# Block-sparse attention with a Fourier mixer: whitened tiles fetched tile by tile, and mask factors kept in memory for TensorE

## The chip, the core and the metric

The kernel runs on one core of one Trainium2 chip. The metric is the time of one execution in device microseconds; three timed runs of the kernel before gave 1060.93, 1061.15 and 1061.73 us, so a median of 1061.15 us. The profile is of one further execution. PE is TensorE's matmul path and PEld its weight loads, DVE is VectorE, ACT is ScalarE, POOL is GpSimd and SP the engine whose queue issues nearly all of the DMAs.

## What is computed

Attention with a block mask over 4 batches, 8 heads, 768 positions and 64 features, and then a mixer over 4 x 768 x 512: a two-dimensional Fourier transform whose real part is added, a normalisation of each row ("whitening"), and two matrix products with a ReLU between them ("channel work").

```python
scores = scale * np.matmul(q, k.transpose(0, 1, 3, 2))
scores = np.where(mask, scores, -1000000000.0)      # blocks of 32: window, edges, 3 sampled
attn = softmax(scores)
x = np.matmul(attn, v) -> (4, 768, 512)
...
X = np.fft.fft(np.fft.fft(x, axis=1), axis=2)
u = x + np.real(X)
un = (u - mean(u)) / np.sqrt(var(u) + 1e-06)
ch = np.maximum(un @ w_ch1, 0.0) @ w_ch2            # 512 -> 2048 -> 512
return u + ch
```

## The kernel before

Attention goes over 16 pairs of heads (4 for each batch); a pair is 6 slots of two units, and a batch is 24 slots, a "phase". A unit is 128 keys against 384 queries for the two heads: 2 score matmuls (L579), a mask, the exponential on ACT (L599, L607) and 2 value matmuls (L653). The profile records each float32 matmul twice, so a slot has 8 records of each line. For the first units, 106 of 192, PE makes the mask itself: 2 more matmuls (L589, one record each) of two bf16 tables of factors, `of_k` and `off_q`, add it to the scores in PSUM. Once `channel_step` has run for the first time `masks["by_pe"]` is false for good; from then on ACT scales and copies the scores (L607) and DVE multiplies the exponentials by a stored mask (L609). The tables' place in the on-chip memory (`factors`) is then used for other things. DVE or POOL also adds up the exponentials for the softmax's denominator (L634, L639), and a group of small steps turns the sums into scaling factors: PE moves them (L738, L751, "N3"), DVE takes the reciprocal (L754) and multiplies the rows of `x` (L766).

The mixer of batch b runs during phase b+1. Its Fourier steps, normalisation and whitening (L956) are small steps in a queue named `apart`, which fill gaps. Whitening gives 6 tiles `un` (2 halves of the 768 positions times 3) of 128 x 512. Each is transposed in 32 x 32 blocks by DVE (L1015) and written to memory (`far`, L1016); after all 6, `un_back` brings them back with 8 DMAs of 192 KB (L1025) into `unT`, so that they stand turned round as a whole. `right` (L1057) then makes four combinations of 128 x 768 on DVE for the channel work, which are held until the planner's time `state["back"]` has passed (a constant `BACK[b]` after the fetch).

Channel work of a batch is a queue `late`: 8 `quad`s, each 7 products of two matmuls (L1103, four records) by the Strassen-Winograd scheme, with sums on DVE (L1108) and ReLUs on ACT (L1112), and four rounds r of outputs, two quads and 6 `channels` to a round. An output round is either 24 matmuls (6 `channels` of 4, 48 records of L1268, with one DVE addition each, L1271) or 21 products of `round_of` (L1211), again Strassen-Winograd; `seven[r]` picks the second where `state["alone"]` was true at the round's first quad, which means that attention stood still (`until`) for the channel work to end. The last round always takes the first form. It is followed by `store` (L1279), 3 or 4 DMAs for each of the 6 tiles of `x`.

Attention of batch b needs the `x` buffers of batch b-2: `place` (L676 on PE, L677 on ACT) writes the first pair of batch b into them, so `until(finished)` runs the whole remaining channel work of b-2 ahead of it. After that there is a stretch of attention without channel work, before the quads of batch b-1 can start (the "dry stretch"). In later pairs `x` is filled by way of memory (`row`, L692, L696).

The instructions of each engine stand in one order, which this program writes as it is built: `when` holds a planned time for each engine, `busy` books work, `gap` fills PE's waits with the first step of `apart` that is due, `do_apart` issues one. SP's DMAs are issued in program order too, and each waits until the one eight before it on SP has landed. Queries and keys (`load_q`, `load_k`, L231) and the turned outputs (L692, L696) go through the same queue.

The lines that the change touches: the tables at L369 to L380, `scores` (L579 to L589), `un_flip` (L998, the last batch alone, which turns its tiles on PE), `un_blocks`, `un_back`, `right`, `quad`'s operands (L1099, L1103), the list `after` of steps of `apart`, `BACK`, `channel_step` and `slot`.

Of the kernel before, what the change touches and what calls it, by code (L numbers as in the profile page):

```python
# [11 lines left out]
FP32 = mybir.dt.float32  # L12
BF16 = mybir.dt.bfloat16
# [86 lines left out]
def kernel(  # L100
# [14 lines left out]
    nc = tc.nc  # L115

    B, H, S, D = q.shape
    DM = H * D
    FF = w_ch1.shape[1]
    P = 128  # L120
    C = S // P
    BLK = 32
    NB = S // BLK
    NR = sampled_blocks.shape[1]
    HS = S // 2
    KS = cos_s.shape[1]
    KD = cos_d.shape[1]
    ND = DM // P
    NF = FF // P
    T = C // 2  # L130
# [51 lines left out]
    tr_p = ctx.enter_context(tc.tile_pool(name="tr_p", bufs=2))  # L182
# [3 lines left out]
    far_p = ctx.enter_context(tc.tile_pool(name="far_p", bufs=1, space=bass.MemoryType.DRAM))  # L186
# [7 lines left out]
    when = {"PE": 0.0, "ACT": 0.0, "DVE": 0.0, "POOL": 0.0}  # L194
# [18 lines left out]
    def room(i, shape, name, dtype=FP32):  # L213
        return big.tile(shape, dtype, tag=f"big{i}", name=name)
# [86 lines left out]
    def bit(n):  # L301
# [5 lines left out]
                      in_=bass.AP(tensor=_words(sampled_blocks, NB * NR), offset=0,  # L307
                                  ap=[[0, NB], [1, 2 * NB * NR]]))
# [30 lines left out]
    factors = room(2, [P, 3, S], "factors", BF16)  # L339
    of_k, off_q, keep_q = (factors[:, i, :] for i in range(3))  # L340
# [5 lines left out]
    def twice(t):  # L346
        nc.vector.tensor_copy(out=t[D:D + NB, :], in_=t[0:NB, :])
# [18 lines left out]
                            op0=ALU.is_equal)  # L366
    spread_q(off_q[0:NB, :], maskT)
    twice(off_q)
    def mask_step(i):  # L369


        half, c = divmod(i, C)
        m, at = ps_m.tile([P, 512], FP32, tag="m", name="m"), bank("m")
        nc.tensor.matmul(m[:, 0:HS], of_k[0:D, c * P:(c + 1) * P],
                         keep_q[0:D, half * HS:(half + 1) * HS], start=True, stop=True)
        done = busy("PE", 0.17) + HOP

        def keep_it():
            nc.scalar.copy(out=mask[:, c, half * HS:(half + 1) * HS], in_=m[:, 0:HS])
            give(at, busy("ACT", 0.5, done))  # L380
        return keep_it
# [62 lines left out]
    for w, w_sb in ((w_ch1, w1_sb), (w_ch2, w2_sb)):  # L444
        rows, cols = w.shape
        words = _words(w, rows * cols)
        for row in range(rows // P):
            for col in range(0, cols, WN):
                src = bass.AP(tensor=words, offset=2 * (row * P * cols + col),
                              ap=[[2 * cols, P], [1, 2 * WN]])  # L450
# [35 lines left out]


    by_pe, to_gather = set(), deque()
    masks = {"by_pe": True}

    turned, e_of, acc_of, o_of, sums_of, x_of, sp_of = {}, {}, {}, {}, {}, {}, {}
    s_at, e_at, e_free, oT_at, acc_at = {}, {}, {}, {}, {}
# [69 lines left out]
    def scores(us):  # L562

        n, w = divmod(us[0], UP)
        half = w // C
        qT, kT = turned[n, 0], turned[n, 1]
        queries = slice(half * HS, (half + 1) * HS)
        got = []
        for u in us:
            c = u % C  # L570
            s = ps_s.tile([P, 2, 512], FP32, tag="s", name="s")
            got.append((u, s))
            if n < NP or masks["by_pe"]:
                by_pe.add(u)
            busy("PE", 0.72, max(e_at.get(u - SLOT, 0.0), z_at[u % 2]))
            s_at[u] = when["PE"] + HOP
            for i in range(2):
                rows = slice(D * i, D * i + D)
                nc.tensor.matmul(s[:, i, 0:HS], kT[rows, c * P:(c + 1) * P], qT[rows, queries],  # L579
                                 start=True, stop=u not in by_pe)  # L580
        for u, s in got:
            if u not in by_pe:
                continue
            c = u % C
            busy("PE", 0.25)
            s_at[u] = when["PE"] + HOP
            for i in range(2):
                rows = slice(D * i, D * i + D)
                nc.tensor.matmul(s[:, i, 0:HS], of_k[rows, c * P:(c + 1) * P], off_q[rows, queries],  # L589
                                 start=False, stop=True)  # L590
        return got

# [390 lines left out]
    def mixer(b, xA, xB):  # L983


        uns, unT = {}, {}
# [2 lines left out]

        def un_flip(half, m):  # L990
            if half not in unT:
                unT[half] = tr_p.tile([P, ND, T * P], FP32, tag="tr", name="unT")
            un = uns.pop((half, m))
            tag, pool = (("t", ps_t), ("m", ps_m))[half == 1 and m != 0]
            tp = pool.tile([P, ND, P], FP32, tag=tag, name="utp")
            for d in range(ND):
                nc.tensor.transpose(tp[:, d, :], un[:, d * P:(d + 1) * P], ident)
            nc.scalar.copy(out=unT[half][:, :, m * P:(m + 1) * P], in_=tp)  # L998

# [3 lines left out]

        lines = {}

        def un_blocks(half, m):  # L1010

            un = uns.pop((half, m))
            if half not in lines:
                lines[half] = far_p.tile([T, P, DM], FP32, tag=f"un{half}", name="far")
            nc.vector.transpose(out=un, in_=un)  # L1015
            nc.sync.dma_start(out=lines[half][m], in_=un)  # L1016

        def un_back():

            for half in range(2):  # L1020
                unT[half] = tr_p.tile([P, ND, T * P], FP32, tag="tr", name="unT")
                of = lines[half].rearrange("m (g j) (k a i) -> a j k (m g) i",
                                           j=BLK, a=P // BLK, i=BLK)
                for a in range(P // BLK):
                    nc.sync.dma_start(  # L1025
                        out=unT[half][BLK * a:BLK * a + BLK].rearrange(
                            "j k (g i) -> j k g i", i=BLK),
                        in_=of[a])
            state["back"] = max(when["PE"], state["ready"]) + BACK[b]

        t, s = {}, {}
        K1, K2 = slice(0, ND // 2), slice(ND // 2, ND)

        def spare_room():
            if s:
                return
            rest, n, w = room(5, [P, ND * HS], "t4"), HS * ND // 2, P * ND // 2
            t[4] = rest[:, 0:n].rearrange("p (k n) -> p k n", n=HS)
            for i in (1, 3, 4):
                s[i] = rest[:, n:n + w].rearrange("p (k n) -> p k n", n=P)  # L1040
                n += w

        def right(j, *tiles):

            spare_room()
            if 1 not in t:
                both = room(4, [P, ND, HS], "t12")
                t[1], t[2], t[3] = both[:, K1, :], both[:, K2, :], unT[1][:, K1, :]
            b11, b21 = unT[0][:, K1, :], unT[0][:, K2, :]
            b12, b22 = unT[1][:, K1, :], unT[1][:, K2, :]  # L1050

            def part(ap):
                return ap.rearrange("p k (t n) -> p k t n", n=P)[:, :, tiles[0]:tiles[-1] + 1, :]

            to, a, c = {1: (t[1], b12, b11), 2: (t[2], b22, t[1]), 3: (b12, b22, b12),
                        4: (t[4], b21, t[2])}[j]
            tt(out=part(to), in0=part(a), in1=part(c), op=ALU.subtract)  # L1057
# [24 lines left out]
        def quad(p):  # L1082

            g = p // 2 % 2 if last else 0
# [11 lines left out]
            l1, l2 = 2 * (p % 2), 2 * (p % 2) + 1  # L1096
            h11, h12, h21, h22 = (hs[g, i][:, l, :] for l in (l1, l2) for i in range(2))
            a11, a12, s2, a22 = blocks(p)
            b11, b21, b22 = unT[0][:, K1, :], unT[0][:, K2, :], unT[1][:, K2, :]  # L1099

            def product(to, a, c, after=0.0):
                for k in range(ND // 2):
                    nc.tensor.matmul(to, a[:, k, :], c[:, k, :], start=(k == 0),  # L1103
                                     stop=(k == ND // 2 - 1))
                return busy("PE", PRODUCT, after) + HOP

# [12 lines left out]
            x, at = ps_m.tile([P, 512], FP32, tag="m", name="xp")[:, 0:HS], bank("m")  # L1119
# [6 lines left out]
            y, at = ps_m.tile([P, 512], FP32, tag="m", name="yp")[:, 0:HS], bank("m")  # L1126
# [272 lines left out]
        le = [("d", lambda i=i: left(0, i), 0.0, 0.0, COMBINE) for i in (1, 3, 4)]  # L1399
# [3 lines left out]
        if not last:  # L1403
            before = first + [pq[1], ar[0][1], ar[1][1], sp[0][1],
                              pq[2], wh[0][1], ft[0][1], ar[0][2], ar[1][2], sp[0][2],
                              pq[0], wh[0][2], ft[0][2], ar[0][0], ar[1][0], sp[0][0],
                              sp[1][1], wh[0][0], ft[0][0], sp[1][2], wh[1][1], ft[1][1],
                              sp[1][0], wh[1][2], ft[1][2], wh[1][0], ft[1][0]]
            after = ([("-", un_back, 0.0, 0.0, 0.0)] + le +
                     [("b", lambda i=i: right(i, 0, 1, 2), 0.0, 0.0, 1.0 if b else 1.7)  # L1410
                      for i in (1, 2, 3, 4)])
        rest = []
        for r in range(2 if last else 0):
            rest += [(lambda p=p: quad(p), 7 * PRODUCT) for p in range(4 * r, 4 * r + 4)]
# [12 lines left out]
    MOST, LEAST = 9.6, 2.5  # L1427
    COVER = 100.0
    AHEAD = 2.2
    BACK = 13.0, 12.0, 15.0  # L1430
    ALONE = 3.0
    LEAVES = 13.0
    SP = UP // SLOT
    SB = SP * NP
    W_PACE = 1.42
    short, apart, late, due = deque(), deque(), deque(), deque()
# [4 lines left out]
             "alone": False, "drain": lambda: None}  # L1441

    def channel_step():
        masks["by_pe"] = False
        late.popleft()[0]()

    def behind(kind):
# [104 lines left out]
    def slot(sl):  # L1552
# [3 lines left out]
        opens = sl % 2 == 0  # L1556
        state["paired"] |= opens and len(late) > 0
        paired = state["paired"]

        def sum_up():  # L1560

# [268 lines left out]
```

## Time and profile before

| what | us |
|---|---|
| median of three timed runs | 1061.15 |
| the profiled execution | 1062.32 |
| span of its instructions | 1060.2 |
| PE busy in it | 1014.9 |
| mean granted clock | 0.986 of full |
| DVE / ACT / POOL busy | 712.8 / 373.2 / 327.3 |

PE works almost all the time; where it doesn't, or where its clock is granted at half, is what the rest of the profile is read for. The costliest groups of DVE around the change, from the part of the page that lists groups of instructions (line, engine, operation, tiles, count | busy us, mean ns of one | idle us before them, released by):

```profile
L609 DVE TENSOR_TENSOR e<-s,mask 128x768 f32<-128x768 f32 x86 | 78.3, 948 | 36.7 <-ACT s L607 31.1
L1108 DVE TENSOR_TENSOR hA<-z,hA 128x384 f32<-128x384 f32 x64 | 35.6, 556 | 67.0 <-PE z L1103 66.9
L766 DVE TENSOR_TENSOR x<-x,r 128x512 f32<-128x512 f32 x24 | 23.0, 996 | 0.1
```

A unit's mask on DVE takes 0.948 us, and 86 units have it. The groups of the DMA part of the page:

```profile
far<-un SPq DMA_DIRECT2D x18, 256.0 KB
unT<-far SPq DMA_DIRECT2D x24, 192.0 KB
qb<-in_q_dram SPq DMA_DIRECT2D x44, 96.0 KB
```

Three batches are fetched back, with 8 DMAs each.

### The profile page before, as it was taken

The page shows a single profiled execution, that of the slowest core. Times are in us where ns is not written, and L with a number is a line of the kernel's source. Part 1 is how long each engine was busy: PE and PEld are TensorE (multiplying, and loading weights), DVE is VectorE, ACT ScalarE, POOL GpSimd, SP SyncE. Part 2 cuts the span into 40 slices and gives each one's busy share as a digit, 9 for nine tenths or more (in the row PEclk, how much of TensorE's full clock was granted, in tenths as well). Part 3 has the DMA queues.
Part 4 walks back from the last instruction along what each step waited for, and adds up shares of the span by engine and source line. Part 5 has one row for each costly group of instructions (what it writes and reads, how often), then busy time and mean ns, then how long its engine had stood idle before and what let it go on. Part 6 is the DMA issues. An engine that isn't in the chain of part 4 may idle for free.

```text
span 1060.2 us, 13059 instructions
## 1 busy us (share of the span) xinstructions
PE 1014.9 (96%) x4526; PEld 564.1 (53%) x4526; DVE 712.8 (67%) x1292; ACT 373.2 (35%) x763; POOL 327.3 (31%) x363
## 2 busy tenths in 40 slices
PE   8999999999999999799999999869999999999996
PEld 4333345435776853344544764334454764578575
DVE  6898795969776567574579477656357575674663
ACT  6978755563122223343241223333120221210210
POOL 1000183565733306373354222743340221000000
PEclk9999999999999999899999999989999999999998
DMA  7857522292000014732120002731000001000001
GB/s 213 233 168 220 113 46 45 50 141 35 1 1 1 1 46 115 104 64 46 30 45 1 1 11 72 137 65 23 11 18 10 1 1 41 19 1 1 0 17 47
DMA packets 163461, 58.12 MB, mean 55 GB/s; under 512 B 144172, under 2 KB 154170, under 8 KB 163386
## 3 DMA queue, kind: packets, MB, share of 16 engines
q1 hardware_dynamic: 162134, 56.45, 23.9%
q8 instruction: 38, 0.62, 0.3%
q10 hardware_dynamic: 1220, 0.72, 0.3%
q14 instruction: 37, 0.30, 0.1%
q0 software_dynamic: 32, 0.01, 0.0%
HBM read 43.80 MB, written 13.37 MB: 54 GB/s over the span
## 4 chain that ended last, share of the span: by engine, by line
PE 82%; DVE 7%; ACT 3%; POOL 2%; DMA 2%; issue 2%; SPq 2%; DVEq 0%; ACTq 0%; POOLq 0%
PE z L1103 16%; PE y L1268 12%; PE s L579 10%; PE o L653 8%; PE yp L1103 8%; PE yy L1336 7%; PE xp L1103 4%; PE yz L1211 3%; PE yw L1211 2%; PE yc L1211 2%; PE zp L861 2%; DVE e L609 1%; POOL acc L639 1%; PE s L589 1%; ACT e L599 1%
## 5 line engine op out<-in xcount | busy, mean ns | idle before, releaser
L639 POOL TENSOR_TENSOR acc<-acc,e 128x384 f32<-128x384 f32 x162 | 165.8, 1056 | 84.8 <-DVE e L609 62.2
L579 PE MATMUL s<-qT,kT 64*128 64x384 f32 x768 | 157.6, 525 | 28.8 <-DVE e L609 22.3
L653 PE MATMUL o<-e,vr 128*64 128x384 f32 x768 | 143.0, 499 | 0.0
L579 PEld LDWEIGHTS s<-qT,kT 64*128 64x128 f32 x768 | 64.7, 188 | 112.2 <-DVE e L609 42.7
L607 ACT ACTIVATE s<-s 128x768 f32<-128x768 f32 x86 | 65.7, 793 | 133.2 <-PE s L579 125.7
L639 POOL TENSOR_TENSOR acc<-e 128x384 f32<-128x384 f32 x40 | 44.7, 1137 | 212.7 <-ACT e L599 125.2
L609 DVE TENSOR_TENSOR e<-s,mask 128x768 f32<-128x768 f32 x86 | 78.3, 948 | 36.7 <-ACT s L607 31.1
L599 ACT ACTIVATE e<-s 128x768 f32<-128x768 f32 x106 | 80.9, 811 | 53.3 <-PE s L589 34.9
L1103 PE MATMUL z<-unT,t 128*128 128x384 f32 x256 | 93.3, 487 | 0.8 <-DVE hA L1108 0.8
L653 PEld LDWEIGHTS o<-e,vr 128*64 128x64 f32 x768 | 48.0, 137 | 71.0 <-issue 68.6
L1108 DVE TENSOR_TENSOR hA<-z,hA 128x384 f32<-128x384 f32 x64 | 35.6, 556 | 67.0 <-PE z L1103 66.9
L1112 ACT ACTIVATE hA<-hA 128x384 f32<-128x384 f32 x64 | 33.5, 523 | 123.4 <-DVE hA L1108 123.4
L1268 PE MATMUL y<-w_sb,hB 128*128 128x512 f32 x168 | 75.2, 596 | 0.0
L1268 PE MATMUL y<-w_sb,hA 128*128 128x512 f32 x168 | 75.1, 595 | 0.0
L1224 POOL TENSOR_TENSOR x<-of,x 128x256 f32<-128x256 f32 x45 | 34.8, 780 | 125.2 <-ACT of L1216 85.2
L1103 PEld LDWEIGHTS z<-unT,t 128*128 128x128 f32 x256 | 48.4, 190 | 35.6 <-DVE hA L1108 2.4
L1271 DVE TENSOR_TENSOR x<-y,x 128x512 f32<-128x512 f32 x42 | 28.9, 688 | 54.8 <-PE y L1268 54.8
L1112 ACT ACTIVATE hB<-hB 128x384 f32<-128x384 f32 x64 | 33.5, 523 | 86.3 <-DVE hB L1108 86.3
L1268 PEld LDWEIGHTS y<-w_sb,hB 128*128 128x128 f32 x168 | 31.1, 190 | 38.8 <-issue 38.6
L1268 PEld LDWEIGHTS y<-w_sb,hA 128*128 128x128 f32 x168 | 31.1, 190 | 37.3 <-issue 36.0
L1103 PE MATMUL xp<-unT,w_sb 128*128 128x384 f32 x128 | 49.9, 515 | 0.0
L1103 PE MATMUL yp<-unT,w_sb 128*128 128x384 f32 x128 | 47.4, 493 | 0.0
(236 smaller groups left out, 1703.8 us busy)
## 6 DMA issues: line engine op xcount, KB each, us to landing
wraw<-in_moe_w_ch_dram SPq DMA_DIRECT2D x32, 512.0 KB
vr<-in_v_dram SPq DMA_DIRECT2D x30, 192.0 KB
far<-un SPq DMA_DIRECT2D x18, 256.0 KB
unT<-far SPq DMA_DIRECT2D x24, 192.0 KB
qb<-in_q_dram SPq DMA_DIRECT2D x44, 96.0 KB
kb<-in_k_dram SPq DMA_DIRECT2D x44, 96.0 KB
out_dram<-x SPq DMA_DIRECT2D x11, 252.0 KB
out_dram<-x SPq DMA_DIRECT2D x18, 128.0 KB
```

The source lines that it names most:

```text
L579: nc.tensor.matmul(s[:, i, 0:HS], kT[rows, c * P:(c + 1) * P], qT[rows, queries], start=True, stop=u not in by_pe)
L599: nc.scalar.activation(out=e, in_=s[:, :, 0:HS], func=ACT.Exp, scale=scale)
L607: nc.scalar.activation(out=s[:, :, 0:HS], in_=s[:, :, 0:HS], func=ACT.Exp, scale=scale)
L609: nc.vector.tensor_tensor(out=e, in0=s[:, :, 0:HS], in1=m.broadcast_to([P, 2, HS]), op=ALU.mult)
L639: nc.gpsimd.tensor_add(out=acc[:, i, :], in0=start[:, i, :], in1=e[:, i, :])
L653: nc.tensor.matmul(o[D * i:D * i + D, :], vt[:, i, c, :], e[:, i, :], start=(c == 0), stop=(c == C - 1))
L1103: nc.tensor.matmul(to, a[:, k, :], c[:, k, :], start=(k == 0), stop=(k == ND // 2 - 1))
L1108: tt(out=to, in0=ps, in1=a, op=ALU.add)
L1112: nc.scalar.activation(out=h, in_=h, func=ACT.Relu)
L1211: nc.tensor.matmul(to, a[:, k, :], c[:, k, :], start=start and k == 0, stop=k == 1, skip_group_check=True)
L1268: nc.tensor.matmul(y, hs[0, half][:, l, m * P:(m + 1) * P], w2_sb[:, 4 * r + l, :], start=(l == 0), stop=(l == 3))
L1336: nc.tensor.matmul(ps, a[:, k, :], c[k // 2][:, k % 2, :] if isinstance(c, list) else c[:, k, :], start=(k == 0), stop=(k == 3))
```

## The change

It has two parts. In the first, each of the 6 whitened tiles has its own place in memory (`lines[half, m]`) and its own 4 fetches of 64 KB (`fetch`), which are issued when the next tile has been written, if fewer than 6 steps of channel work are left in `late`; what is left is fetched by `un_back`. `unT` is laid out tile by tile (`[P, T, ND, P]`), and `right` runs in 8 pieces: tiles 1 and 2 together, then tile 0. `BACK` no longer depends on the batch: 9.0 after the last fetch for tiles 1 and 2, and 2.0 more for tile 0 (`un_last`).

In the second, the two tables of factors (384 KB) are stored to memory at slot 4. When a slot of phase 2 or 3 begins and `late` is empty, `mask_factors` loads them back into a buffer that is free then (`room(2)`), and while the planner's time for PE is beyond that load by `FACTORS` (4.0), `scores` makes masks on PE again. Every `channel_step` ends this, and a later dry stretch loads them anew.

As built, the order of instructions has these differences. In batch 0's mixer the first quad comes before the last attention slot, N3 (L751) directly ahead of it, and its first output round is in L1268's form instead of 21 products. In batch 1 all 24 fetches come together after the last `far` write, ahead of the stores of the first half (L1279); the attention around them has no PE masks, and the quads begin sooner after the last output round. In batch 2 the fetches come by fours between other DMAs, the last 8 together, then the one load of the factors, then queries; 10 units have PE masks, and the first quad comes two slots earlier. The last batch has only the new layout.

```diff
+    far_factors = far_p.tile([P, 2, S], BF16, tag="factors", name="far")
+    masks = {"by_pe": True, "at": 0.0, "of_k": of_k, "off_q": off_q}
+
+    def mask_factors():
+
+        again = room(2, [P, 3, S], "factors", BF16)
+        nc.sync.dma_start(out=again[:, 0:2, :], in_=far_factors)
+        masks.update(at=when["PE"] + FACTORS, of_k=again[:, 0, :], off_q=again[:, 1, :])
+
...
-                nc.tensor.matmul(s[:, i, 0:HS], of_k[rows, c * P:(c + 1) * P], off_q[rows, queries],
+                nc.tensor.matmul(s[:, i, 0:HS], masks["of_k"][rows, c * P:(c + 1) * P],
+                                 masks["off_q"][rows, queries],
                                  start=False, stop=True)
...
-        lines = {}
+        lines, sent = {}, deque()
+
+        def fetch(half, m):
+            if half not in unT:
+                unT[half] = tr_p.tile([P, T, ND, P], FP32, tag="tr", name="unT")
+            of = lines[half, m].rearrange("(g j) (k a i) -> a j k g i",
+                                          j=BLK, a=P // BLK, i=BLK)
+            for a in range(P // BLK):
+                nc.sync.dma_start(
+                    out=unT[half][BLK * a:BLK * a + BLK, m, :, :].rearrange(
+                        "j k (g i) -> j k g i", i=BLK),
+                    in_=of[a])
 
         def un_blocks(half, m):
 
             un = uns.pop((half, m))
-            if half not in lines:
-                lines[half] = far_p.tile([T, P, DM], FP32, tag=f"un{half}", name="far")
+            lines[half, m] = far_p.tile([P, DM], FP32, tag=f"un{half}{m}", name="far")
             nc.vector.transpose(out=un, in_=un)
-            nc.sync.dma_start(out=lines[half][m], in_=un)
+            nc.sync.dma_start(out=lines[half, m], in_=un)
+            while sent and len(late) < 2 * T:
+                fetch(*sent.popleft())
+            sent.append((half, m))
 
         def un_back():
 
-            for half in range(2):
-                unT[half] = tr_p.tile([P, ND, T * P], FP32, tag="tr", name="unT")
...
-            state["back"] = max(when["PE"], state["ready"]) + BACK[b]
+            while sent:
+                fetch(*sent.popleft())
+            state["back"] = max(when["PE"], state["ready"]) + BACK[0]
+
+        def un_last():
+
+            state["back"] += BACK[1]
...
-            after = ([("-", un_back, 0.0, 0.0, 0.0)] + le +
-                     [("b", lambda i=i: right(i, 0, 1, 2), 0.0, 0.0, 1.0 if b else 1.7)
-                      for i in (1, 2, 3, 4)])
+            on = [[("b", lambda i=i, m=m: right(i, *m), 0.0, 0.0, us) for i in (1, 2, 3, 4)]
+                  for m, us in (((1, 2), 1.2), ((0,), 0.7))]
+            after = ([("-", un_back, 0.0, 0.0, 0.0)] + le + on[0] +
+                     [("-", un_last, 0.0, 0.0, 0.0)] + on[1])
...
-    BACK = 13.0, 12.0, 15.0
+    BACK = 9.0, 2.0
     ALONE = 3.0
+    FACTORS = 4.0
...
     def channel_step():
-        masks["by_pe"] = False
+        masks.update(by_pe=False, at=None)
         late.popleft()[0]()
...
+        if sl == 4:
+            nc.sync.dma_start(out=far_factors, in_=factors[:, 0:2, :])
+        if phase > 1 and not late:
+            if masks["at"] is None:
+                mask_factors()
+            masks["by_pe"] = when["PE"] > masks["at"]
```

More of the change, by code (lines that the diff above doesn't have):

```diff
@@ L488 @@
     by_pe, to_gather = set(), deque()
-    masks = {"by_pe": True}
     turned, e_of, acc_of, o_of, sums_of, x_of, sp_of = {}, {}, {}, {}, {}, {}, {}
@@ L997, in un_flip @@
                 nc.tensor.transpose(tp[:, d, :], un[:, d * P:(d + 1) * P], ident)
-            nc.scalar.copy(out=unT[half][:, :, m * P:(m + 1) * P], in_=tp)
-        lines = {}
+            nc.scalar.copy(out=unT[half][:, m, :, :], in_=tp)
+        lines, sent = {}, deque()
+        def fetch(half, m):
+            if half not in unT:
+                unT[half] = tr_p.tile([P, T, ND, P], FP32, tag="tr", name="unT")
+            of = lines[half, m].rearrange("(g j) (k a i) -> a j k g i",
[5 more added lines that the diff above has]
+                    in_=of[a])
@@ L1018, in un_back @@
+            sent.append((half, m))
         def un_back():
-            for half in range(2):
[L1021 to L1028, printed above, removed]
@@ L1029, in un_back, with by_k @@
-            state["back"] = max(when["PE"], state["ready"]) + BACK[b]
+            while sent:
[3 more added lines that the diff above has]
+            state["back"] += BACK[1]
         t, s = {}, {}
         K1, K2 = slice(0, ND // 2), slice(ND // 2, ND)
+        def by_k(half, ks):
+            return unT[half][:, :, ks, :].rearrange("p m k n -> p k m n")
         def spare_room():
@@ L1037, in spare_room @@
             rest, n, w = room(5, [P, ND * HS], "t4"), HS * ND // 2, P * ND // 2
-            t[4] = rest[:, 0:n].rearrange("p (k n) -> p k n", n=HS)
+            t[4] = rest[:, 0:n].rearrange("p (k m n) -> p k m n", m=T, n=P)
             for i in (1, 3, 4):
@@ L1045, in right @@
             spare_room()
+            b11, b21, b12, b22 = (by_k(h, ks) for h in range(2) for ks in (K1, K2))
             if 1 not in t:
[L1047 to L1050, printed above, removed]
+                both = room(4, [P, ND, T, P], "t12")
+                t[1], t[2], t[3] = both[:, K1], both[:, K2], b12
             def part(ap):
-                return ap.rearrange("p k (t n) -> p k t n", n=P)[:, :, tiles[0]:tiles[-1] + 1, :]
+                return ap[:, :, tiles[0]:tiles[-1] + 1, :]
             to, a, c = {1: (t[1], b12, b11), 2: (t[2], b22, t[1]), 3: (b12, b22, b12),
@@ L1098, in quad @@
             a11, a12, s2, a22 = blocks(p)
-            b11, b21, b22 = unT[0][:, K1, :], unT[0][:, K2, :], unT[1][:, K2, :]
+            b11, b21, b22 = by_k(0, K1), by_k(0, K2), by_k(1, K2)
             def product(to, a, c, after=0.0):
                 for k in range(ND // 2):
-                    nc.tensor.matmul(to, a[:, k, :], c[:, k, :], start=(k == 0),
+                    nc.tensor.matmul(to, a[:, k, :], c[:, k], start=(k == 0),
                                      stop=(k == ND // 2 - 1))
```

## The prediction

> **What bounds the kernel now.** I read the page from the top, then windows of 20 us, then the PE timeline where a window is not full, then the queues of the engines named as releasers.
>
> ```profile
> PE 1014.9 (96%) x4526; PEld 564.1 (53%) x4526; DVE 712.8 (67%) x1292; ACT 373.2 (35%) x763; POOL 327.3 (31%) x363
> ```
>
> PE is busy for 1014.9 of 1060.2 us, so an edit pays only through the 45.3 us in which PE idles, through half clock, or through less PE work. The windows show where the idle time sits away from the start and the end:
>
> ```profile
> 420.00:440.00 20.00, 12.69 (x67) 4.69 (x67) 13.88 (x16) 8.44 (x13) 13.79 (x14) 0.98 0.91 128
> 440.00:460.00 20.00, 19.85 (x74) 9.58 (x76) 12.73 (x19) 6.93 (x16) 7.71 (x8) 0.85 0.32 70
> 680.00:700.00 20.00, 10.30 (x54) 3.98 (x54) 12.48 (x15) 6.72 (x11) 11.37 (x13) 0.80 0.76 113
> ```
>
> The columns are the window, its length, busy time of PE, PEld, DVE, ACT and POOL, granted clock, DMA share and GB/s. Both places are the dry stretches: attention without channel work, before the first quad of batch 1 and of batch 2. The PE timeline there, first around 430, then around 690:
>
> ```profile
> 419.90 1.78 PE L579 MATMUL s<-qT,kT 64*128 64x384 f32 x8 [1.68 <-DVE e L609]
> ...
> 429.48 1.78 PE L579 MATMUL s<-qT,kT 64*128 64x384 f32 x8 [1.29 <-DVE e L609]
> 431.18 2.80 PE L653 MATMUL o<-e,vr 128*64 128x384 f32 x16
> 440.15 2.93 PE L579 MATMUL s<-qT,kT 64*128 64x384 f32 x8 [6.17 <-DVE e L609]
> 443.01 2.93 PE L1103 MATMUL xp<-unT,w_sb 128*128 128x384 f32 x4
> ```
> ```profile
> 673.17 1.78 PE L579 MATMUL s<-qT,kT 64*128 64x384 f32 x8 [1.69 <-DVE e L609]
> ...
> 682.74 1.78 PE L579 MATMUL s<-qT,kT 64*128 64x384 f32 x8 [1.29 <-DVE e L609]
> ...
> 697.93 2.93 PE L579 MATMUL s<-qT,kT 64*128 64x384 f32 x8 [8.40 <-DVE e L609]
> ```
>
> Small waits for DVE's mask product, then one long wait in each, and scores at half clock behind it (2.93 instead of 1.56 us). What DVE, ACT and SP did in the long waits:
>
> ```profile
> 420.49 11.31 SPq L1025 DMA_DIRECT2D unT<-far  x8
> 431.90 3.03 SPq L231 DMA_DIRECT2D qb<-in_q_dram  x4
> ```
> ```profile
> 435.54 0.96 DVE L1057 TENSOR_TENSOR t<-unT 128x768 f32<-128x768 f32 x1 [5.26 <-DMA unT<-far]
> ...
> 438.21 0.84 ACT L536 ACTIVATE qT<-qb 128x768 f32<-128x768 f32 x1 [6.12 <-DMA qb<-in_q_dram]
> ```
> ```profile
> 691.76 0.84 ACT L536 ACTIVATE qT<-qb 128x768 f32<-128x768 f32 x1 [6.40 <-DMA qb<-in_q_dram]
> ```
>
> The eight fetches hold SP for 11.31 us and land 15.0 us after the first is issued (420.49 to 435.5). DVE stands in `right` behind them, the mask product behind `right`, and the queries for ACT stand behind the fetches on SP.
>
> **The change part by part** (us against the profiled span). The order of both programs on each engine is known; the planner has moved more than the edit names. For PE I write S4, O4, Y4, T4 and P3 for the groups that stand in rows of L579 (8 records, 1.39 at pitch), L653 (8, 1.43), L1268 (8, 3.45), L738 (0.78) and L676 (0.38).
>
> *A, batch 0 loses one Strassen round.* Its first quad now starts one attention slot earlier, with attention left over, so it is not "alone" and outputs r=0 take the L1268 form (48 records), not 21 L1211 products. Rows: the three `round_of` from 263.23 to 281.84 are 18.6; 16 records of L1268 take 7.03, 6.97 at pitch, so 48 take 20.9. +2.3 (2.0 to 2.6).
>
> *B, one mask group fewer there*: 4 records of L589, 0.42 at pitch. -0.4.
>
> *C, VectorE at that quad.* The sums of the quad (L1108) now stand behind the reciprocal and five scalings (L766) that wait for N3 (L751), which moved just ahead of the quad. Quad at 242.89 - 3.25 (one slot) + 0.45 = 240.1; its fifth product, four products of 1.29 and the first weight load later, 245.4. DVE: 240.1 + 0.44 + five scalings + 0.56. At their mean of 0.996 that is 246.1, so +0.7; at the least, 0.68, it is hidden (0); at 1.71, as the two at 254.5 beside POOL, 249.6, so +4.2. I take the mean since POOL's adds of two slots are only partly alongside.
>
> *D, batch 1.* Fetching starts when fewer than six channel pieces are left; here all 24 fetches still go out together, behind the last `far` write and ahead of the four stores of half 0. Batch 2's placing copy (L677 on ACT) must wait until these stores have read their buffer, and the exponentials are queued behind that copy on ACT. With t0 the end of the first output group of r=3 (386.05 before): fetches from t0+2.8 for 11.3 (the same bytes and descriptors by the row above), stores 4.53 behind them (four took that at 392.31), so the copy at about t0+19; copy 0.48, scaling 0.80, mask 0.95 and hops, PE's third scores at t0+22.3. PE has Y8 6.9, S4, P3, S4, O4 until about t0+12.9: 9.4 idle, then about 2.5 lost to half clock. Behind it S4, Y4, T4, Y8 (12.5): quad at t0+37.3. What this leaves for later, seven score and six value groups, is 18.3, and I keep one mask wait of 1.2: 56.8. Before: 443.01 - 386.05 = 57.0, less the Fourier steps that moved ahead (2.0), plus 1.5 of half clock inside the first product: 56.5. +0.3; from -9.0 (no such wait) to +4 (stores slower by as much as the fetches' landing, 15.0 against 11.3). Masks by PE are never reached in this phase.
> On 24 pieces of 64 KB: the Trainium skill, "SBUF — State Buffer", section "The DMA setup-cost knee", says about 2 us fixed for each transfer and that a loop of 64 KiB tiles runs at 30% of the rate of big ones. The run before shows 105 GB/s even at 192 KB (1.57 MB in 15.0 us). Were the 24 strictly one after another, 24 x 2.15 = 52 us, an estimate from that page, D would be some 35 us worse; SP's waits keep eight in flight, and then it is 6.5, under SP's own 11.3.
>
> *E, batch 2.* Tiles 1 to 4 are fetched early, the last two together, then the factors (384 KB) once, then queries. Ten units have PE masks and the quad is two slots earlier. To gain: 1.29 + 8.40 idle and 1.37 + 0.67 of half clock (697.93 and 700.79 rows against 1.56 and 2.80): 11.7. Five L589 groups cost 2.1. But the first waits in PE's order, with the rest of attention behind it, for the factors: last `far` at 672.0, eight fetches to 676.2, load at 676.3, landed at about 680 (3 to 4.5 us as for the last of the old fetches); PE arrives at 674.9: 5.1 idle and about 2.0 at half clock. -11.7 + 2.1 + 7.0 = -2.6; bounds -9.6 (landed in time) and +1 (landed four later).
>
> *F, the store of the factors* at the fourth slot: one more issue on SP (0.34 as `far`), in the start's busy traffic. +0.3 (0 to 1). Eight `right` of 0.69 and 0.42 instead of four of 0.95 cost 0.6 on DVE, hidden in both dry stretches by PE's work, and in batch 0 by the time before N3.
>
> Sum: 2.3 - 0.4 + 0.7 + 0.3 - 2.6 + 0.3 = +0.6, to 1060.8 of span. The profiled run took 1062.32, the median of timed runs is 1061.15 (1060.93 to 1061.73); I add to the median: 1061.8. Stalls move rather than go.
>
> A rule weighed in D and E: the Trainium skill, "TensorE: Matmul & The Clock Gate", section "Part 1: The HAM clock gate", gives half clock after an idle window of about 3.4 us that runs freely. In the trace the drop came 5.4 us into one wait and 2.5 into the other, and lasted until 446 and 702. By the rule the 5.1 us wait in E might pass without a drop, and E would be -4.6.
>
> **Rivals.**
> - *R1, faster: the copy is not held by the fetches.* For it: before, L677 at 398.87 waited only 1.54. Against it: the stores' place in SP's order. D becomes -9.0: 1061.8 - 9.3 = 1052.5.
> - *R2, faster: the factors are there in time.* For it: DMA share is 0.76 in 680 to 700, not full, and half of the fetches go earlier. Against: 1.4 us between issue and need. E -9.6 in place of -2.6: 1054.8.
> - *R3, slower: VectorE late at batch 0's first quad.* From five scalings slower than about 0.9 each it decides; at 1.71 the wait is 4.2, with a clock drop of 2.0: 1061.8 + 3.5 + 2.0 = 1067.3. For it: `right` took 1.56 to 1.76 beside POOL at 238 to 245. Against: the median of all scalings is 0.75.
> - *R4, slower: it doesn't do what it says.* PE masks come only for ten units, and if their factors land after 683 nothing is won: E 0 to +1, so 3.1 above the forecast: 1064.9.
>
> **How the numbers follow.** Forecast 0.36 (own range 1058 to 1065), R1 0.17, R2 0.16, R3 0.19, R4 0.12. 0.2% is 2.1 us, about what can be told from no change. The forecast splits 0.07 faster, 0.20 same, 0.09 slower; with the rivals 0.40, 0.20, 0.40. The range takes in R1 to R3: 1052 to 1068.
>
> **What would show it.** A: 336 instead of 420 records of L1211, and r=0 over in 20.9. C: PE waiting for L1108 near 245. D: a PE wait of about 9 us some 13 us into the last round, ACT's L677 released by a DMA. E: PE's first late L589 waiting for a DMA for about 5 us. I am wrong if the first D wait is under 3 us, if the factors have landed, or if time goes elsewhere than these stretches.

## The result and the profile after

The changed kernel takes 1080.28 us (median of four runs, 1079.74 to 1082.1) against 1061.26 us of the kernel before on the same chip: a ratio of 1.0182, 95% interval 1.0164 to 1.0200. It is 19 us slower; the forecast was 1061.8 us, about the same, in a range of 1052 to 1068. The profiled execution took 1079.74 us with a span of 1078.0 us, 17.8 us more than before.

The page's first part for the changed kernel:

```profile
PE 1016.6 (94%) x4506; PEld 556.9 (52%) x4506; DVE 706.0 (65%) x1285; ACT 368.8 (34%) x754; POOL 305.0 (28%) x342
```

PE is busy for 1.7 us more than before (1014.9). The other 16.1 us are idle time of PE. 13.2 of them sit in the two places that the prediction watched (8.6 in batch 1, 4.6 in batch 2), about 2.3 at the first quad of batch 0. Windows of 20 us of the changed kernel (PE, PEld, DVE, ACT, POOL, clock, DMA share, GB/s):

```profile
400.00:420.00 20.00, 3.73 (x21) 1.35 (x19) 1.82 (x2) 1.62 (x4) 3.85 (x4) 0.75 0.57 100
420.00:440.00 20.00, 17.55 (x47) 7.47 (x48) 13.47 (x17) 5.30 (x10) 7.43 (x6) 0.83 0.18 38
680.00:700.00 20.00, 5.89 (x32) 2.17 (x31) 5.54 (x8) 2.84 (x9) 7.28 (x9) 0.74 0.59 137
```

In 400 to 420 no engine works for more than 4 of 20 us, and the DMA engines are little over half busy. That they could move more shows in shorter windows, the first two of the changed kernel, during the fetches and during the four stores behind them, the third of the kernel before, during its fetches:

```profile
406.00:410.00 4.00, 0.00 (x0) 0.00 (x0) 0.00 (x0) 0.00 (x0) 0.00 (x0) 0.98 0.62 97
414.60:418.00 3.40, 0.00 (x0) 0.00 (x0) 0.00 (x0) 0.00 (x0) 0.00 (x0) 0.50 0.79 167
```
```profile
424.00:428.00 4.00, 4.00 (x24) 1.43 (x20) 3.17 (x5) 2.07 (x3) 3.62 (x5) 1.00 0.91 123
```

The small fetches move 97 GB/s at a DMA share of 0.62, the large ones of the same bytes 123 GB/s at 0.91. So the wait is for the issuing queue, not for the DMA engines. The PE timeline of the changed kernel at these places (line numbers of the new file: L587 is the old L579, L597 the mask on PE, L618 the mask on DVE, L686 the placing copy, L1124 the quad's products):

```profile
401.27 1.78 PE L587 MATMUL s<-qT,kT 64*128 64x384 f32 x8 [0.77 <-DVE e L618]
402.98 1.51 PE L662 MATMUL o<-e,vr 128*64 128x384 f32 x8
422.36 2.93 PE L587 MATMUL s<-qT,kT 64*128 64x384 f32 x8 [17.87 <-DVE e L618]
...
685.80 1.78 PE L587 MATMUL s<-qT,kT 64*128 64x384 f32 x8 [1.69 <-DVE e L618]
701.17 0.82 PE L597 MATMUL s<-factors 64*128 64x384 bf16 x4 [13.59 <-DMA factors<-far]
```

One wait of 17.87 us in batch 1, one of 13.59 us in batch 2. Both are the waits that the prediction named in D and E, with the releasers that it named; it gave them 9.4 and 5.1 us. What SP and ACT did, first in batch 1:

```profile
394.14 0.35 SPq L1035 DMA_DIRECT2D far<-un  x1
394.58 19.97 SPq L1025 DMA_DIRECT2D unT<-far  x24
414.66 2.50 SPq L1300 DMA_DIRECT2D out_dram<-x  x4
```
```profile
419.31 0.48 ACT L686 COPY x<-xt 128x384 f32<-128x384 f32 x1 [18.38 <-DMA out_dram<-x]
```

The 24 fetches hold SP for 19.97 us, not 11.3. The four stores of the first half stand behind them, the placing copy on ACT waits for the stores, the exponentials stand behind the copy. Then SP in batch 2:

```profile
682.53 0.35 SPq L1035 DMA_DIRECT2D far<-un  x1
682.99 4.99 SPq L1025 DMA_DIRECT2D unT<-far  x4
688.09 2.31 SPq L1300 DMA_DIRECT2D out_dram<-x  x3
690.50 1.01 SPq L271 DMA_DIRECT2D vr<-in_v_dram  x2
691.61 0.37 SPq L1035 DMA_DIRECT2D far<-un  x1
692.03 5.37 SPq L1025 DMA_DIRECT2D unT<-far  x8
697.44 0.62 SPq L375 DMA_DIRECT2D factors<-far  x1
```
```profile
683.86 0.71 DVE L1034 STREAM_TRANSPOSE un<-un 128x512 f32<-128x512 f32 x1
```

From 682.53 to 698.06 SP issues without a pause worth the name. The last tile is transposed by 684.57 (the DVE line), but its write leaves at 691.61, and the load of the factors at 697.44, ten microseconds after PE first needed them (687.6).

### The profile page after: what moved, and what is told of

The parts are those of the page before. It is cut to its first block, busy times and chain, and to the rows that moved or that the text cites. A ratio compares the mean times of both kernels' runs of the same rounds, so it can differ in the third digit from the quotient of the medians.

```text
span 1078.0 us, 13008 instructions
## 1 busy us (share of the span) xinstructions
PE 1016.6 (94%) x4506; PEld 556.9 (52%) x4506; DVE 706.0 (65%) x1285; ACT 368.8 (34%) x754; POOL 305.0 (28%) x342
## 3 DMA queue, kind: packets, MB, share of 16 engines
q1 hardware_dynamic: 163190, 57.24, 22.3%
## 4 chain that ended last, share of the span: by engine, by line
PE 79%; DVE 9%; SPq 3%; ACT 3%; issue 2%; DMA 2%; POOL 1%; ACTq 0%; DVEq 0%
PE z L1124 15%; PE y L1289 14%; PE s L587 9%; PE o L662 8%; PE yp L1124 7%; PE yy L1357 6%; PE xp L1124 4%; PE yz L1232 3%; SPq L1025 2%; PE yw L1232 2%; PE zp L870 2%; PE yc L1232 2%; DVE t L1078 1%; ACT e L608 1%; PE s L597 1%
## 5 line engine op out<-in xcount | busy, mean ns | idle before, releaser
L587 PE MATMUL s<-qT,kT 64*128 64x384 f32 x768 | 155.7, 520 | 28.8 <-DVE e L618 22.1
L587 PEld LDWEIGHTS s<-qT,kT 64*128 64x128 f32 x768 | 64.4, 188 | 110.6 <-DVE e L618 35.0
L608 ACT ACTIVATE e<-s 128x768 f32<-128x768 f32 x114 | 86.9, 811 | 75.4 <-PE s L597 52.3
L618 DVE TENSOR_TENSOR e<-s,mask 128x768 f32<-128x768 f32 x78 | 71.0, 950 | 60.0 <-ACT s L616 53.7
L616 ACT ACTIVATE s<-s 128x768 f32<-128x768 f32 x78 | 59.1, 791 | 106.9 <-PE s L587 106.7
L1124 PE MATMUL z<-unT,t 128*128 128x384 f32 x256 | 93.1, 486 | 1.7 <-DVE hA L1129 1.7
L1289 PE MATMUL y<-w_sb,hB 128*128 128x512 f32 x192 | 86.4, 601 | 0.0
L1289 PE MATMUL y<-w_sb,hA 128*128 128x512 f32 x192 | 85.3, 595 | 0.0
L1292 DVE TENSOR_TENSOR x<-y,x 128x512 f32<-128x512 f32 x48 | 33.1, 690 | 60.5 <-PE y L1289 60.5
L1124 PEld LDWEIGHTS z<-unT,t 128*128 128x128 f32 x256 | 48.6, 190 | 36.0 <-DVE hA L1129 2.3
L1289 PEld LDWEIGHTS y<-w_sb,hB 128*128 128x128 f32 x192 | 36.0, 192 | 46.2 <-issue 45.7
L1289 PEld LDWEIGHTS y<-w_sb,hA 128*128 128x128 f32 x192 | 35.8, 190 | 44.1 <-issue 41.7
L1245 POOL TENSOR_TENSOR x<-of,x 128x256 f32<-128x256 f32 x36 | 26.3, 736 | 95.6 <-ACT of L1237 65.5
L1124 PE MATMUL xp<-unT,w_sb 128*128 128x384 f32 x128 | 47.5, 493 | 0.0
L1144 ACT COPY hA<-xp 128x384 f32<-128x384 f32 x32 | 15.3, 478 | 92.5 <-PE xp L1124 92.4
```

The costliest lines, as they stand in the source:

```text
L608: nc.scalar.activation(out=e, in_=s[:, :, 0:HS], func=ACT.Exp, scale=scale)
L616: nc.scalar.activation(out=s[:, :, 0:HS], in_=s[:, :, 0:HS], func=ACT.Exp, scale=scale)
L618: nc.vector.tensor_tensor(out=e, in0=s[:, :, 0:HS], in1=m.broadcast_to([P, 2, HS]), op=ALU.mult)
L1124: nc.tensor.matmul(to, a[:, k, :], c[:, k], start=(k == 0), stop=(k == ND // 2 - 1))
L1289: nc.tensor.matmul(y, hs[0, half][:, l, m * P:(m + 1) * P], w2_sb[:, 4 * r + l, :], start=(l == 0), stop=(l == 3))
```

## The experiments

In each, "the change" is the changed kernel, and times are compared with the kernel before on the same chip (1061.0 to 1061.2 us).

**1. The stores ahead of the fetches in batch 1.** The 24 fetches go out when three steps of channel work are left instead of six.

```diff
-            while sent and len(late) < 2 * T:
+            while sent and len(late) < (T + 1 if b == 1 else 2 * T):
...
-        hold = 2 * T
+        hold = T if b == 1 else 2 * T
```

> In batch 1 the 24 fetches stand behind the four stores of the first half instead of ahead of them; the order of PE is unchanged. Theory (SP is held about 20 us by the 24 fetches wherever they stand): the wait of 17.9 us before the third scores goes, because the stores and with them the placing copy come early, but the fetches end later, so the first quad of batch 1 waits for the combinations instead, about 8 us: 1068 to 1073 us. Rival (only the order of stores and fetches costs): no new wait, 1060 to 1063 us. Rival (DMA traffic as a whole): no gain, 1078 or more.

1064.47 us, ratio 1.0035 (1.0023 to 1.0047): 15.8 us of the 19 are gone. SP in this run:

```profile
398.43 4.54 SPq L1300 DMA_DIRECT2D out_dram<-x  x4
403.06 17.45 SPq L1025 DMA_DIRECT2D unT<-far  x24
```

The fetches hold SP nearly as long (17.45 us against 19.97), but the attention no longer stands behind them: the third scores wait 1.61 us instead of 17.87 (first line below). The new wait that I expected at the quad is there, though small, since the combinations on DVE began at 420.07, as the tiles landed, and PE had output work until 421.9:

```profile
408.63 1.78 PE L587 MATMUL s<-qT,kT 64*128 64x384 f32 x8 [1.61 <-DVE e L618]
...
423.06 1.56 PE L1124 MATMUL xp<-unT,w_sb 128*128 128x384 f32 x4 [1.16 <-DVE x L1292]
425.24 1.56 PE L1124 MATMUL yp<-unT,w_sb 128*128 128x384 f32 x4 [0.62 <-ACT hA L1144]
```

So the time, between my theory and its rival, speaks for the order as the price in batch 1: the same fetch time, moved behind four stores of 4.54 us, costs 1.8 us of waiting at the quad, and 1.6 in place of 17.9 at the scores. In batch 2 this run still waits 14.05 us for the factors.

**2. The factors loaded earlier, in phases 2 and 3.** The load is issued with the last channel step rather than with the next slot.

```diff
         masks.update(by_pe=False, at=None)
         late.popleft()[0]()
+        if not late and state["phase"] in (2, 3):
+            mask_factors()
...
+        state["phase"] = phase
```

> The load of the factors is issued as soon as the last channel step is out, ahead of the values and of the last 8 fetches, instead of behind them (there is one more load in phase 2 that nothing uses); PE's order is unchanged. Theory (the load waits in SP's queue): it lands about 7 us sooner, PE's wait of 13.6 us becomes 5 to 7, 1071 to 1074 us. Rival (the transfer itself is slow): within 2 us of 1080.

1079.99 us, ratio 1.0177 (1.0158 to 1.0195): no gain in time, as the rival had it, but not for the rival's reason. The wait for the factors in batch 2 fell from 13.59 to 6.58 us, as the theory had it, and a new wait of 4.26 us came at the first quad of phase 2, with half clock behind it. The next run shows where that one comes from.

**3. Both.** Edits 1 and 2 together.

> Stores first and factors early together. If the two waits are independent the gains add: 1060 to 1066 us by the theory; 1052 to 1055 by the rival that only the order costs.

1070.86 us, ratio 1.0090 (1.0065 to 1.0115): slower than edit 1 alone, by 6.4 us. The gains do not add, and neither number was met. PE of this run in phase 2 (first line) and in phase 3, then ACT in phase 2:

```profile
439.83 2.93 PE L1124 MATMUL z<-unT,t 128*128 128x384 f32 x4 [10.28 <-DVE hA L1129]
...
693.67 0.82 PE L597 MATMUL s<-factors 64*128 64x384 bf16 x4 [6.72 <-DMA factors<-far]
```
```profile
438.71 0.48 ACT L1144 COPY hA<-xp 128x384 f32<-128x384 f32 x1 [27.22 <-DMA factors<-far]
```

In phase 3 the wait for the factors fell from 14.05 to 6.72 us, as the theory had it. In phase 2 the load, which no mask uses there, goes into the buffer that the next quad's `hA` needs (`room(2)` is both), and the quad waits 10.28 us for a transfer that nothing reads. It is the wait of 4.26 us of run 2. That was a fault of the experiment.

**4. The early load in phase 3 only,** with edit 1 (`state["phase"] == 3`).

> Stores first in batch 1, and the load of the factors issued with the last channel step in batch 2 alone, so that no load in phase 2 holds the buffer of the first quad there. Theory (two waits in SP's queue that are independent): batch 2's wait falls from 14.0 to 6.7 us as in the run before, and the 10.3 us at the quad of batch 1 are gone: 1056 to 1060 us. Rival (the extra load in phase 2 cost nothing, the gain is lost elsewhere): 1068 or more.

1056.83 us, ratio 0.9955 (0.9940 to 0.9971). The wait for the factors is 5.64 us. With the stray load gone the two waits are independent, and the sum is met: the first version faster than the kernel before.

**5. The factors ahead of one more tile's fetch,** with edits 1 and 4. The four fetches that went out behind the fifth tile's write are put off; they now go out with the last eight, behind the last write. By the code (a tile is fetched when the next has been written) and by the count of fetches they are the fourth tile's, not the fifth's, as the expectation calls them.

```diff
-            while sent and len(late) < 2 * T:
+            while sent and len(late) < (T + 1 if b == 1 else 2 * T) and not (b == 2 and len(late) == 1):
```

> As the run with the early load in batch 2, and the fifth tile of batch 2 is fetched behind the factors instead of ahead of them (12 fetches together at the end). PE's order is unchanged. Theory (SP's issue time ahead of the load is all of the wait): the load goes out some 5 us sooner, the wait for it falls to 0 to 3 us; the last fetches land some 2 us later for the combinations and the queries: 1049 to 1056 us, the fastest of all. Rival (the wait goes to the first quad or to the queries of the next pair, which stand behind 12 fetches): 1058 to 1062 us.

1054.03 us, ratio 0.9933 (0.9920 to 0.9947). SP and PE of this run:

```profile
669.08 0.85 SPq L375 DMA_DIRECT2D factors<-far  x1
670.03 3.19 SPq L271 DMA_DIRECT2D vr<-in_v_dram  x2
```
```profile
676.05 0.82 PE L597 MATMUL s<-factors 64*128 64x384 bf16 x4 [4.45 <-DMA factors<-far]
```

The load now leaves before PE needs it (671.6), and still 4.45 us of waiting are left: from the start of its issue to its use it takes 7.0 us, against 3.7 in the changed kernel and 3 to 4.5 in the prediction. So what is left is the time from issue to landing, not the queue ahead of the load. The DMA engines were busy then (a share of 0.97 in 671.6 to 673); whether that made the load slower was not tried.

**6. Masks on PE begin two slots later,** with edit 5 (`FACTORS` 8.0 for 4.0). Six units of batch 2 have PE masks, instead of ten.

> As the run with the factors first, with FACTORS at 8.0 instead of 4.0, so that the first two slots of batch 2's dry stretch still have DVE masks and three have PE masks. Theory (the wait of 4.5 us for the factors is for the first masks alone): no wait for the factors and one of 1 to 3 us for DVE, 1050 to 1053 us. Rival (the wait only changes its name): 1053 to 1056 us.

1048.80 us, ratio 0.9889 (0.9873 to 0.9905): the fastest version, just below the theory's range. PE there:

```profile
678.00 1.78 PE L587 MATMUL s<-qT,kT 64*128 64x384 f32 x8 [0.97 <-DVE e L618]
679.62 0.49 PE L597 MATMUL s<-factors 64*128 64x384 bf16 x4
```

The first mask on PE waits for nothing; two slots with DVE masks bridge the transfer at 0.97 us of waiting. PE also has two groups of masks less, 0.8 us. The constant 4.0 is a planned time on PE that stands for a transfer which takes longer, behind a queue that the planner does not book.

**7. No factors at all,** once with the change's order and once with edit 1: the tile-by-tile fetch alone, all masks after the start on DVE.

> The whitened tiles are fetched one by one as in the change, but the factors are neither stored nor loaded back, and DVE makes all masks after the start. Theory (SP's queue is the bound of the dry stretch, with or without the factors): the wait for the factors gives way to one for DVE and the queries of 8 to 12 us, 1074 to 1080 us. Rival (the price in batch 2 is that of the factors alone): the wait goes altogether, 1066 to 1068 us.

1073.27 us, ratio 1.0109 (1.0091 to 1.0127), just below the range of the theory. The dry stretch has its old kind of waits (2.69 and 5.29 us for DVE) in place of 13.59: as built, the masks on PE cost 7.0 us.

> Stores first in batch 1, and no factors and no PE masks after the start: the fetching alone, with its order mended. Theory (the two stretches add): 1064.5 less the 7.0 us that leaving out the factors gave before, 1056 to 1059 us, so that the tile-by-tile fetch alone is worth 2 to 5 us and the masks on PE 2 to 5 more when their factors come in time. Rival (PE masks carry the whole gain): 1061 or more.

1056.67 us, ratio 0.9955 (0.9941 to 0.9969): the waits add up as forecast (1064.5 less 7.0 is 1057.5). The fetch alone, in a better order, is worth 4.5 us, and run 6, with masks on PE and their factors in time, is 7.9 us below that. Not all of the 7.9 need be the masks': run 6 also puts off one tile's fetch, and no run without PE masks does.

**8. The masks alone, on the kernel before.** The 8 large fetches stay; the factors are stored and loaded as in the change; 14 units in each dry stretch have PE masks.

> The second part of the change alone on the kernel before: 8 fetches of 192 KB as before, and PE masks for 14 units in each of the two dry stretches from factors loaded behind the fetches. Theory (the first PE mask waits for a load that stands behind the fetches on SP): a wait of about 14 us in each dry stretch in place of 7.5 and 9.7, and 2.9 us of masks each: 1072 to 1080 us. Rival (masks on PE take DVE off the path and pay for themselves): 1045 to 1058 us.

1081.40 us, ratio 1.0193 (1.0178 to 1.0209), 1.4 us beyond the theory's range and far from the rival. PE in batch 1:

```profile
436.95 0.82 PE L597 MATMUL s<-factors 64*128 64x384 bf16 x4 [16.76 <-DMA factors<-far]
```

The load stands behind 11.11 us of fetches, and PE waits 16.76 us (16.36 in batch 2), where DVE's masks had let it run on for three more slots (four in batch 2) before its long wait. With their load behind the fetches the masks on PE harm by themselves; the small fetches are not needed for that.

**9. The first output round of batch 0 as 21 products again,** in the change.

```diff
-                    seven[p // 2] = state["alone"] and p // 2 < NF // 4 - 1
+                    seven[p // 2] = (state["alone"] or b == 0 and len(late) > 0) and p // 2 < NF // 4 - 1
```

> The change, with the first output round of batch 0 in its form of 21 products again. PE's order changes with it: batch 1's fetches come spread, and phase 2 has a dry stretch with PE masks as phase 3 has. Theory (SP's order sets both stretches): 2.3 us of PE work saved, the 17.9 us of waiting for the stores go down to some 5, and a wait of 10 to 14 us for the factors comes in phase 2: 1070 to 1081 us. Rival (the lost round upset the plan, and with it back the change does what it is for): 1045 to 1058 us.

1089.72 us, ratio 1.0269 (1.0253 to 1.0284): beyond the theory's range, and far from the rival. Phase 2 now has the dry stretch, with a wait of 15.06 us for the factors, on top of 1.65 and 3.47 us for DVE masks behind a late placing copy; in batch 2 the wait for the factors is still there (13.79). PE idles 66.6 us in all, against 61.4 in the change. So the lost round does not explain the slowness: the plan that it leads to avoids one of these waits. What the round itself costs is read from its rows (2.0 us, see *A* below); this run can't part it from the plan.

**10. All 24 fetches of batch 2 together,** with the early load and edit 1.

> As the run with the factors first, but all 24 fetches of batch 2 go out together behind the last write, as the planner does in batch 1. Theory (each fetch holds SP about 0.65 us, wherever it stands): 8 us more of SP behind the factors, of which the queries and the combinations for the first quad take 4 to 9 us: 1058 to 1063 us. Rival (fetching early is worth nothing): 1053 to 1056 us.

1056.35 us, ratio 0.9955 (0.9940 to 0.9970): just outside both ranges, 2.3 us slower than run 5. The factors leave earlier, and their wait is 1.76 us instead of 4.45. Against that the quad waits 3.97 us in its third product, at half clock afterwards. SP, ACT and PE there:

```profile
670.84 17.11 SPq L1025 DMA_DIRECT2D unT<-far  x24
688.05 2.27 SPq L231 DMA_DIRECT2D qb<-in_q_dram  x4
```
```profile
692.68 0.84 ACT L544 ACTIVATE qT<-qb 128x768 f32<-128x768 f32 x1 [7.17 <-DMA qb<-in_q_dram]
```
```profile
694.37 2.93 PE L1124 MATMUL z<-t,w_sb 128*128 128x384 f32 x4 [3.97 <-ACT e L608]
```

The product writes a buffer that scores use too, and the exponential that frees it stands on ACT behind the queries, which stand on SP behind the 24 fetches. The combinations are not what it waits for: they start at 687.39 and are done by 691.5. Fetching early is worth the difference of the two waits and the half clock, less than I had put it.

## Why the prediction was wrong

The failed step is a term of the sum that was mis-sized: SP's time for the fetches. The prediction took "the same bytes and descriptors by the row above", 11.3 us for 24 fetches, because 8 fetches of the same bytes had taken 11.31. In place of that SP was held for 19.97 us. From the trace of before, one fetch of 192 KB holds SP for 0.646 to 2.449 us, 1.291 in the median; in the trace of after, one of 64 KB for 0.557 to 1.721, 0.635 in the median. A third of the bytes takes half the time, not a third: 24 x 0.635 is 15.2 us, the second to the fifth of batch 1 took 1.43 to 1.72 each (3.7 us more), and 1.0 us lies between the issues, which makes 19.97.

*D* by its own times: with t0 at 391.5 the fetches start at t0+3.1 (forecast 2.8) and PE runs dry at t0+13.0 (12.9). The copy comes at t0+27.8 instead of 19, the third scores at t0+30.9 instead of 22.3. The difference, 8.6 to 8.8 us, is that of SP's 19.97 and 11.3; the stores behind the fetches held SP 2.0 us less than forecast (2.50 against 4.53), but the copy came 2.2 us after the last of them was issued, so these two nearly cancel. The mechanism was right to the instruction, and run 1 shows it by taking it away. PE's idle time in the stretch went from 10.0 to 18.6 us; D was forecast at +0.3 and is about +8.

*E* had the same mistake and an omission. Set against the scores at 673.17 before and 685.80 after, the last write should have left at 684.6; it left at 691.61, because the four fetches behind the fifth tile's write (4.99), three stores (2.31) and two loads of values (1.01) stood ahead of it on SP. Of these the sum held nothing. Then the write and the last eight fetches took 5.8 us instead of 4.3, and the load was in use 3.7 us after its issue began, as assumed: 13.6 us of waiting instead of 5.1. Runs 1, 4, 5 and 6 took the wait away piece by piece (14.05, 5.64, 4.45, none), so it was the queue, and in the end the time from issue to landing. E was forecast at -2.6; by idle time (0.91 + 1.69 + 13.59 + 0.74 = 16.9 against 12.3), five mask groups (2.1) and half clock (about 0.6 more) it is +7.3.

*A* is +2.0 (264.02 to 284.62, 20.6 against 18.6; forecast 2.3). *C*: PE waits 1.73 us for the sums of the quad, and 2.01 us for N3's own input before it, against 1.4 us of smaller waits for DVE and POOL around batch 0's quads that went: +2.3, forecast 0.7 with 4.2 as its bound.

```profile
240.37 0.55 PE L760 MATMUL st<-ident,sums 128*128 128x128 f32 x3 [2.01 <-DVE sums L717]
...
247.81 1.56 PE L1124 MATMUL z<-unT,t 128*128 128x384 f32 x4 [1.73 <-DVE hA L1129]
```
```profile
242.04 1.74 DVE L643 TENSOR_TENSOR acc<-acc,e 128x768 f32<-128x768 f32 x1
243.71 0.45 DVE L763 RECIPROCAL r<-st 128x48 f32<-128x48 f32 x1
244.19 3.10 DVE L775 TENSOR_TENSOR x<-x,r 128x512 f32<-128x512 f32 x5
```

The five scalings took 3.10 us together, less than the 5.0 assumed. What was late was their start: the prediction had the reciprocal at the quad's start (240.1), and it came at 243.7, behind the combinations, which took up to 1.5 us each, and an addition of exponentials of 1.74. With B (-0.4) the terms make 19.2. That agrees with the same instruction in both runs behind the second stretch (L1695 at 755.18, now L1724 at 774.71, 19.5 us later) and with the 19.0 of the medians. The spans of the two profiled runs differ by 17.8 only, because the run of before had half clock at 903 to 907, 1.7 us for two groups of L1103, and that of after had not.

Of the rivals, *R4* was the nearest in kind (the masks on PE win nothing in time), at 1064.9 us; its bound of 1 us for a late load was far too small, since how late the load came hung on all that stood ahead of it on SP. *R1* is what run 1 built by hand: the wait gone, 15.8 us less. *R2* is near to run 6, and there the gain is real. *R3* came in part: VectorE was late at batch 0's first quad, by 1.73 us of its 4.2, but not because of slow scalings, and the clock did not drop there.

The sentence from the Trainium skill, "SBUF — State Buffer", section "The DMA setup-cost knee", spoke against small pieces, and I set it aside as 6.5 us, under SP's own time. Its direction was right. Its figure does not explain the loss: about 2 us fixed for each transfer, eight in flight, is 6 us over 24 pieces, an estimate from that page, while SP was held 17 to 20 us. What the traces here show is the time on the issuing queue.

On the clock, the windows agree with the forecast: half clock behind the long waits, 0.75 and 0.83 in 400 to 440, 0.74 and 0.83 in 680 to 720, worth 2 to 3 us at each place. Whether a wait of 5.1 us would have passed without a drop a wait of 13.59 can't show; in run 5 one of 4.45 us did not (granted clock 0.50 in 676 to 678).

## What to carry to other kernels

A transfer that is cut into pieces can cost its issuing queue more for the same bytes (here 17 to 20 us in 24 pieces, 11 in 8), and everything that stands behind it in program order pays for that. So measure one issue of the very shape, and then list what is queued behind it, to the last engine that waits: here a store, a copy, an exponential and PE. An operation moved to a faster engine pays only when its operands are there; start it at the first use that the transfer can meet (run 6), not as soon as the plan has room. Before a buffer is loaded early, look who else lives in it: an unused load cost 10 us of waiting (run 3).

## What was not expected of the hardware

The issue time of one fetch of 64 KB was not constant: in batch 1 the second to the fifth of 24 took 1.43 to 1.72 us each, the other twenty 0.58 to 0.64; four that went out at 682.99 took 4.99 us, and four at 669.02 took 2.61. What makes the slow ones slow stays open; no run was made for it. A fetch of several tiles in one piece in the new layout was not tried either.
